# A fused attention and feed-forward block: the end of the last tile re-ordered, four shared head groups, and gb folded into the down weights

## The chip, the cores and the metric

The kernel runs on one core of a Trainium2 chip. A core has five engines that run their own instruction streams and wait for each other through semaphores: TensorE (PE; its weight loads are listed as PEld), VectorE (DVE), ScalarE (ACT), GpSimd (POOL) and SyncE (SP), whose queue (SPq) issues most of the DMA transfers; ACT has a DMA queue of its own (ACTq). Matmul results land in PSUM, eight banks of 128 x 512 fp32; all else is kept in SBUF. The metric is device time in microseconds (us) for one execution, and the median of several executions is compared.

## The reference

One sequence of 2048 tokens of 512 features, 32 heads of 16 features, a gated feed-forward part of width 1792:

```
mod = silu(c) @ w_mod              -> sa, ca, ga, sb, cb, gb   (512 each)
h = layernorm(x) * (1 + ca) + sa
q, k, v = h @ wqkv                 (32 heads of 16)
x = x + ga * (softmax(q k^T / 4) v) @ wo
h = layernorm(x) * (1 + cb) + sb
x = x + gb * ((gelu(h @ w_gate) * (h @ w_up)) @ w_down)
```

B_x is not used. Inputs and output are bf16; the layernorm's epsilon is 1e-5.

## The kernel before

**Work.** The 2048 queries are cut into seven sets of 512, 512, 256, 256, 256, 128 and 128 (`SETS`, numbered 0 to 6). The 32 heads form eight groups of four, called quads (`qd`). One unit of attention is a quad with the queries of a set; it runs over the 2048 keys in rounds, and each round gives four PSUM banks of scores, 512 columns each. All units together make 2048 banks. The exponential of every bank is taken either by ACT (tile `E`, one instruction for two or three banks of `ps_sc`) or, for some banks, by VectorE with a polynomial on integers (tiles `dt`, `dx`, `ed`, `mreg`, `qT`: a load of one bank out of PSUM, then six steps for one or two banks at a time). The product with the values accumulates in `ps_pv`; a column of ones in `vaug` yields the softmax's denominators.

**Units at the end.** Sets 5 and 6 have 128 queries each. Their first `QS` = 5 quads run as shared units of 256 queries; then come the remaining quads of set 5 alone, then those of set 6 alone. When a unit is done, `pv_done` copies the sums to `osb`. Its denominators normally go through DRAM (osb to `scr_den`, to `den`, a reciprocal in `rden`, to `scr_rec`, and broadcast back into `rb`), four DMAs on SP's queue, after which VectorE writes `onorm`. For the last quads of sets 5 and 6 the denominators are instead spread by a matmul with `self32`, and VectorE takes the reciprocal from PSUM (`near_end`, `tail_den`).

**Order.** The file is a recorder and a planner: `stream` walks through the score banks, keeps ACT fed, and places between them the products with the values, "side work" (`plan`, `next_side`: projections, the modulation vectors, the output projection `side_wo` and the feed-forward part `side_ffn` of finished sets) and VectorE's tasks (`task`, `step`). Waits and the order on each engine follow from this table of instructions. A bank goes to VectorE only under several conditions in `stream`, one of them an upper bound on `credit`, the amount of side work that is owed. Where PE has nothing to do, filler matmuls on `kme` and `ident` are issued.

**Feed-forward.** `side_ffn` handles a set's 14 slices of the width in chunks: for a set of 128 queries four chunks of 4, 4, 4 and 2 slices. A chunk is a gate product, an ACT step (Tanh in the stream, Gelu in the tail), an up product, and VectorE's product into `prodT` (in `hreg`). The down product sums 14 matmuls of 512 columns in one bank. `down_fin` multiplies the sum by the broadcast row `gb`, adds it to `xs`, and SP issues the output DMA of the tile. Of set 5, the first `EARLY` = 2 chunks are made in the stream.

**The tail.** After the last Exp, `tail` merges several generators by which is ready first: the last products with the values (`rest`), the denominators of the last quads, `tail_end` (set 6: output projection `wo_mm` on top of `xs`, layernorm statistics, rstd on POOL, the normalized tile in `dx`, four transposes, `modulate` on ACT and DVE into `wreg`, and its whole feed-forward part) and `tail_ffn` for what is left of set 5. In it the down products of set 5 go to `ps_pv`, those of set 6 to `ps_mi`.

The recorder makes an instruction that reads a PSUM bank wait for an earlier read of the same bank by another engine:

```python
                        elif kind == "ps":
                            for s, n in rd.items():
                                if s != eng:
                                    need(s, n, False)
```

## Time and profile before

| | us |
|---|---|
| median of 3 runs | 896.17 |
| lowest and highest of them | 896.01 and 898.0 |
| the profiled execution | 895.93 |
| its span, from the first to the last instruction | 894.2 |
| ACT busy | 865.8 |
| DVE busy | 816.4 |
| PE busy | 811.3 |
| POOL busy | 19.2 |
| ACT's last Exp starts | 870.97 |
| DVE's last instruction starts | 891.54 |

The granted clock of TensorE was 1.0 over the whole span. A row of the timeline gives the start, the time until the last of the row's instructions ends, the engine, the line, the operation and its output and inputs, how many there are, and in brackets how long the engine was idle before and for whom. A row that merges several pipelined instructions is shorter than their number times the duration of one. A row of the groups gives the busy time, the mean duration of one in ns, and the idle time before. In the order listings, a row is an instruction of one engine in program order, "xN" counts equal neighbours, and the brackets name the engines or DMA semaphores that it waits for.

### The profile page before, as it was taken

The page shows a single profiled execution, that of the slowest core. Times are in us where ns is not written, and L with a number is a line of the kernel's source. Part 1 is how long each engine was busy: PE and PEld are TensorE (multiplying, and loading weights), DVE is VectorE, ACT ScalarE, POOL GpSimd, SP SyncE. Part 2 cuts the span into 40 slices and gives each one's busy share as a digit, 9 for nine tenths or more (in the row PEclk, how much of TensorE's full clock was granted, in tenths as well). Part 3 has the DMA queues.
Part 4 walks back from the last instruction along what each step waited for, and adds up shares of the span by engine and source line. Part 5 has one row for each costly group of instructions (what it writes and reads, how often), then busy time and mean ns, then how long its engine had stood idle before and what let it go on. Part 6 is the DMA issues. An engine that isn't in the chain of part 4 may idle for free.

```text
span 894.2 us, 19936 instructions
## 1 busy us (share of the span) xinstructions
PE 811.3 (91%) x8661; PEld 286.7 (32%) x8661; DVE 816.4 (91%) x1500; ACT 865.8 (97%) x736; POOL 19.2 (2%) x36
## 2 busy tenths in 40 slices
PE   8899999988898898989999898999999999998998
PEld 3333222222222222222233222333333343334455
DVE  7778999999998999999998999998999999979955
ACT  4999999999999999999999999999999999999992
POOL 2100000000000000000000000000000000000000
PEclk9999999999999999999999999999999999999999
DMA  9012122000200000000000000010000000000100
GB/s 305 2 25 70 41 78 60 25 14 14 55 14 8 7 13 14 14 8 19 19 26 14 9 14 9 14 31 19 10 14 21 14 14 8 27 14 9 27 9 12
DMA packets 32509, 25.10 MB, mean 28 GB/s; under 512 B 16233, under 2 KB 28262, under 8 KB 32422
## 3 DMA queue, kind: packets, MB, share of 16 engines
q1 hardware_dynamic: 30566, 22.79, 8.6%
q8 instruction: 67, 1.10, 0.5%
q10 hardware_dynamic: 1856, 1.05, 0.4%
q14 instruction: 20, 0.16, 0.1%
HBM read 21.23 MB, written 2.61 MB: 27 GB/s over the span
## 4 chain that ended last, share of the span: by engine, by line
ACT 91%; PE 6%; DVE 2%; DMA 1%; issue 0%; SPq 0%
ACT E L321 88%; PE ps_sc L308 3%; ACT wreg L321 3%; PE ps_mi L308 2%; PE ps_pv L308 1%; DMA mreg<-in_w_mod_dram 1%; DVE st L361 0%; ACT hreg L321 0%; DVE dt L333 0%; DVE kmo L333 0%; DVE mreg L325 0%; DVE mreg L338 0%; SPq L371 0%; DVE hreg L325 0%; DVE wreg L338 0%
## 5 line engine op out<-in xcount | busy, mean ns | idle before, releaser
L321 ACT ACTIVATE E<-ps_sc 128x1536 bf16<-128x1536 f32 (+2 forms) x698 | 841.7, 1411 | 9.9 <-PE ps_sc L308 9.6
L308 PE MATMUL ps_sc<-qT,kme 32*128 32x256 bf16 (+2 forms) x1600 | 171.0, 304 | 13.8 <-ACT E L321 10.4
L308 PE MATMUL ps_sc<-qT,kmo 32*128 32x256 bf16 (+2 forms) x1664 | 172.2, 298 | 11.1 <-ACT E L321 7.9
L308 PE MATMUL ps_pv<-E,vaug 128*17 128x256 bf16 (+2 forms) x2884 | 179.8, 300 | 2.3 <-DVE osb L342 1.3
L333 DVE TENSOR_SCALAR dt<-ps_sc 128x512 int32<-128x512 f32 x204 | 139.0, 686 | 11.3 <-PE ps_sc L308 8.2
L308 PE MATMUL ps_sc<-kme,ident 128*128 128x512 bf16 x327 | 104.4, 384 | 36.9 <-ACT E L321 33.4
L308 PE MATMUL ps_mi<-wreg,mreg 128*128 128x256 bf16 (+2 forms) x624 | 123.6, 309 | 8.2 <-DVE wreg L342 4.0
L308 PEld LDWEIGHTS ps_sc<-qT,kmo 32*128 32x128 bf16 x1664 | 50.3, 92 | 120.2 <-ACT E L321 72.3
L308 PEld LDWEIGHTS ps_sc<-qT,kme 32*128 32x128 bf16 x1600 | 48.6, 92 | 125.2 <-ACT E L321 74.7
L308 PEld LDWEIGHTS ps_pv<-E,vaug 128*17 128x17 bf16 x2884 | 53.5, 88 | 96.8 <-issue 83.8
L325 DVE TENSOR_TENSOR qT<-qT,dx 128x1024 f16<-128x1024 f16 (+1 forms) x106 | 70.3, 664 | 1.3
L333 DVE TENSOR_SCALAR dx<-dt 128x1024 f16<-128x1024 uint16 (+1 forms) x107 | 70.0, 654 | 0.1
L308 PEld LDWEIGHTS ps_mi<-wreg,mreg 128*128 128x128 bf16 x624 | 47.7, 97 | 63.1 <-issue 30.1
L308 PE MATMUL ps_mi<-dreg,hreg 128*128 128x512 bf16 x210 | 65.3, 385 | 1.5 <-DVE wreg L338 0.8
L338 DVE SCALAR_TENSOR_TENSOR qT<-dt,qT 128x1024 int16<-128x1024 int32 (+1 forms) x53 | 62.3, 1176 | 0.1
L308 PEld LDWEIGHTS ps_sc<-kme,ident 128*128 128x128 bf16 x327 | 23.4, 97 | 88.1 <-ACT E L321 83.4
L325 DVE TENSOR_TENSOR ed<-ed,dx 128x1024 f16<-128x1024 f16 (+1 forms) x72 | 47.7, 662 | 0.7
L342 DVE CAST wreg<-ps_mi 128x512 bf16<-128x512 f32 x51 | 35.0, 686 | 11.3 <-PE ps_mi L308 10.8
L338 DVE SCALAR_TENSOR_TENSOR ed<-dt,ed 128x1024 int16<-128x1024 int32 (+1 forms) x36 | 42.2, 1172 | 0.2
L308 PE MATMUL ps_mi<-hreg,wreg 128*128 128x512 bf16 x120 | 38.7, 385 | 0.8 <-DVE vaug L342 0.5
L338 DVE SCALAR_TENSOR_TENSOR wreg<-wreg,ps_mi 128x512 bf16<-128x512 bf16 x51 | 34.7, 680 | 2.4 <-ACT wreg L321 1.8
L308 PE MATMUL ps_pv<-qT,vaug 128*17 128x256 bf16 (+2 forms) x178 | 36.5, 290 | 0.0
(126 smaller groups left out, 712.9 us busy)
## 6 DMA issues: line engine op xcount, KB each, us to landing
rb<-scr_rec SPq DMA_DIRECT2D x16, 256.0 KB
rb<-scr_rec SPq DMA_DIRECT2D x29, 128.0 KB
mreg<-in_w_mod_dram SPq DMA_DIRECT2D x1, 2048.0 KB, 12.9
out_dram<-xs SPq DMA_DIRECT2D x16, 128.0 KB, 1.7
mreg<-in_B_w_gate_dram SPq DMA_DIRECT2D x4, 448.0 KB, 7.2
mreg<-in_B_w_up_dram SPq DMA_DIRECT2D x4, 448.0 KB, 6.7
dreg<-in_B_w_down_dram SPq DMA_DIRECT2D x3, 512.0 KB, 7.6
wreg<-in_A_wqkv_dram SPq DMA_DIRECT2D x3, 384.0 KB, 9.8
```

The source lines that it names most:

```text
L308: return self.rec("pe", lambda e: e.matmul(out, lhsT, rhs, start=start, stop=stop, tile_position=tp), [lhsT, rhs], [out], cost=(n, int(rhs ...
L321: return self.rec("act", lambda e: e.activation(out, in_, func, scale=scale, **kw), rd, wr, cost=self.cost("act", out, [in_], "act" if bia ...
L325: return self.rec(eng, lambda e: e.tensor_tensor(out, a, b, op), [a, b], [out], cost=self.cost(eng, out, [a, b], "tt"))
L333: return self.rec(eng, lambda e: e.tensor_scalar(out, a, s1, s2, **kw), rd, [out], cost=self.cost(eng, out, [a], "ts" if len(rd) == 1 else ...
L338: return self.rec("dve", lambda e: e.scalar_tensor_tensor(out, a, s, b, op0=op0, op1=op1), rd, [out], cost=self.cost("dve", out, [a, b], " ...
L342: return self.rec(eng, lambda e: e.tensor_copy(out, in_), [in_], [out], cost=self.cost(eng, out, [in_], "ts"))
```

## The change

- `QS` goes from 5 to 4: four shared quads, so sets 5 and 6 have four units of their own each instead of three. `EARLY` goes from 2 to 3: three of the four chunks of set 5 are made in the stream.
- `gb` is multiplied into the down weights once (`scale_wd`, 7 VectorE instructions on `dreg`, a new entry of side work). `down_fin` then is one addition of the bank to `xs`; the tile `xw` is gone; 16 multiplications and 16 additions become 15 additions (the last tile has none).
- Banks may go to VectorE above the bound on `credit` where the next side work has nothing to issue.
- The tail: generators of set 6's chain and of set 5's down products are preferred by `FIRST` = 120 of the planner's ns until set 6's first Gelu, and put back by as much after it. The down products of set 5's first three chunks have a generator of their own (`tail_early`).
- In `tail_end` the epsilon is added by VectorE, POOL only does the power; the normalized tile is made from `xs` instead of the PSUM bank; the transposes alternate between two banks so that ACT reads one and VectorE the other.
- Set 6's down product is made in two halves of 256 columns in two banks (`ps_mi` and one of `ps_sc`); each starts with a matmul of `ident` with `xs`, so that the sum holds the residual. VectorE copies one half out and SP issues its DMA; ACT copies the other and issues its DMA on its own queue.

```diff
-QS = 5
+QS = 4
-EARLY = 2
+EARLY = 3
+FIRST = 120
...
+    def ln_pow(self, a, b):
+        r = self.rstd[:, a:b]
+        v, h = self.mv[:, a:b, 1], self.half[:, 0:b - a]
+        self.rec("pool", lambda e: e.tensor_tensor(r, v, h, ALU.pow), [v, h], [r], cost=self.cost("pool", r, [v], "pow"))
...
+    def scale_wd(self):
+
+        yield from self.until("wd")
+        if not self.dry:
+            self.task([lambda f=f: self.tt("dve", self.wd[:, f:f + 2, :], self.wd[:, f:f + 2, :],
+                                           self.gb[:, :].rearrange("p (o n) -> p o n", o=1).broadcast_to([P, 2, D]), ALU.mult)
+                       for f in range(0, NFC, 2)], "wds")
...
-            self.tt("dve", self.xs[:, t, :], self.xs[:, t, :], self.xw[:, :], ALU.add)
+            self.tt("dve", self.xs[:, t, :], self.xs[:, t, :], bank, ALU.add)
...
-        return [lambda: self.tt("dve", self.xw[:, :], bank, self.gb[:, :], ALU.mult), add]
+        return [add]
...
+        w.append((self.scale_wd, at(160), at(160)))
...
-                        and len(mem) == CH and slack > -100 and self.credit < (2600 if pos < ends[-3] else 1600)):
+                        and len(mem) == CH and slack > -100 and (self.credit < (2600 if pos < ends[-3] else 1600) or (pos >= ends[0] and self.next_side() is None))):
...
+            ahead = FIRST if ("g", kb, 0) not in self.have else -FIRST
...
-                    x = self.probe(nxt[i])
-                    if best is None or max(x, t + 30) < best[0]:
-                        best = max(x, t + 30), i
+                    x = max(self.probe(nxt[i]), t + 30)
+                    if best is None or x < best[0] - (ahead if i >= len(gens) - 2 else 0):
+                        best = x, i
...
-        self.task(self.ln2_steps(k, bank), ("ln2", k), self.after([("s2e", k)]), first=True)
+        v = self.mv[:, tile:tile + 1, 1]
+        steps = self.ln2_steps(k)
+        steps[0] = ("pool", lambda: self.ln_pow(tile, tile + 1))
+        self.task([lambda: self.ts("dve", v, v, EPS, None, ALU.add)] + steps, ("ln2", k), self.after([("s2e", k)]), first=True)
...
-        for h in range(2):
-            pb = f[1 + h]
-            yield lambda h=h, pb=pb: self.transp(pb, lambda t: self.normed(k, t), 1, h)
-            for i in range(2):
-                dc = 2 * h + i
-                self.modulate("act" if i == 0 else "dve", self.t2T[:, dc, c0:c0 + W],
-                              pb.bitcast(BF16)[:, W * i:W * i + W], self.modB, dc)
-        yield from self.tail_ffn(k, self.mi[:, :], f, 4, None)
+        pb = [f[1 + i].bitcast(BF16) for i in range(2)]
+
+        def trans():
+            for dc in range(NDC):
+                self.transpose(pb[dc % 2][:, W * (dc // 2):W * (dc // 2) + W], self.normed(k, 0)[:, P * dc:P * dc + P], self.ident[:, :])
+        yield trans
+        for dc in range(NDC):
+            self.modulate("act" if dc % 2 == 0 else "dve", self.t2T[:, dc, c0:c0 + W],
+                          pb[dc % 2][:, W * (dc // 2):W * (dc // 2) + W], self.modB, dc)
+        down = [self.mi[:, 0:D // 2], l[0][:, 0:D // 2]]
+        for i in range(2):
+            yield lambda i=i: self.mm(down[i], self.ident[:, :], self.xs[:, tile, D // 2 * i:D // 2 * i + D // 2], start=True, stop=False)
+        yield from self.tail_ffn(k, down, f, 4, None)
+
+    def tail_early(self, k, kb, down):
+        n = 512 // SETS[k][1]
+        yield from self.until(("osb", kb, 7))
+        for ci in range(EARLY):
+            yield from self.until(("prod", k, ci))
+            for fc in range(n * ci, min(NFC, n * ci + n)):
+                yield lambda fc=fc: self.down_mm(down, BCOL[k] // P, fc)
+        self.done(("early", k))
...
+        def fin(eng, i, queue, sem):
+            cols = slice(D // 2 * i, D // 2 * i + D // 2)
+            dst = self.xs[:, tile, cols]
+            if eng == "act":
+                self.act(dst, down[i], ACT.Copy)
+            else:
+                self.copy(eng, dst, down[i])
+            if self.probing is None:
+                self.dma(queue, self.out[0, P * tile:P * tile + P, cols], dst, sem)
+        self.task([lambda: fin("dve", 0, "sp", "out3")], None, first=True)
+        self.task([("act", lambda: fin("act", 1, "act", "out2"))], None, first=True)
```

Three places show how the instructions move. First PE after the last quad's denominators begin, before the change (`ps_sc<-wo,onorm` is the output projection of the last tile, `ps_pv<-dreg,hreg` the down product of set 5, `ps_sc<-wreg,mreg` gate and up products, `ps_sc<-ident,dx` the transposes):

```order
L308 MATMUL ps_sc<-wo,onorm 128x512 x2
L308 MATMUL ps_sc<-wo,onorm 128x512 [waits dve]
L308 MATMUL ps_sc<-osb,self 128x128 [waits dve]
L308 MATMUL ps_sc<-wo,onorm 128x512 [waits dve]
L308 MATMUL ps_pv<-dreg,hreg 128x512 x7
L308 MATMUL ps_sc<-wo,onorm 128x512 [waits dve]
L308 MATMUL ps_pv<-dreg,hreg 128x512
L308 MATMUL ps_sc<-wreg,mreg 128x128 x40
L308 MATMUL ps_sc<-wreg,mreg 128x128 [waits act]
L308 MATMUL ps_sc<-wreg,mreg 128x128 x7
L308 MATMUL ps_pv<-dreg,hreg 128x512 [waits dve]
L308 MATMUL ps_pv<-dreg,hreg 128x512 x3
```

And the same stretch of PE in the changed kernel:

```order
L309 MATMUL ps_sc<-wo,onorm 128x512 x2
L309 MATMUL ps_sc<-osb,self 128x128 [waits dve]
L309 MATMUL ps_sc<-wo,onorm 128x512 [waits dve]
L309 MATMUL ps_sc<-wo,onorm 128x512
L309 MATMUL ps_sc<-wreg,mreg 128x128 x16
L309 MATMUL ps_pv<-dreg,hreg 128x512
L309 MATMUL ps_sc<-wo,onorm 128x512 [waits dve]
L309 MATMUL ps_pv<-dreg,hreg 128x512 x11
L313 MATMUL ps_sc<-ident,dx 128x128 [waits dve]
L313 MATMUL ps_sc<-ident,dx 128x128 x3
L309 MATMUL ps_mi<-xs,ident 128x256
L309 MATMUL ps_sc<-xs,ident 128x256
```

The denominator matmul `ps_sc<-osb,self` stands one output projection earlier, 16 gate and up products of set 5 are left instead of 48, 11 of its down products stand between the last output projection and the transposes, and two matmuls with `xs` are new.

Second, VectorE at the same place, before (`st` and `mv` are the statistics of the last tile, `dx` its normalized rows, `hreg<-ps_sc,E` the products of set 5's chunks):

```order
L345 RECIPROCAL rb<-ps_sc 128x128 [waits pe]
L325 TENSOR_TENSOR onorm<-osb,rb 128x128 [waits dve]
L361 BN_STATS st<-ps_sc 128x6 [waits pe]
L364 BN_AGGR mv<-st 128x2 [waits dve]
L338 SCALAR_TENSOR_TENSOR hreg<-ps_sc,E 128x4x128 [waits act,pe]
L333 TENSOR_SCALAR dx<-ps_sc,mv,rstd 128x512 [waits pool,dve]
L338 SCALAR_TENSOR_TENSOR hreg<-ps_sc,E 128x2x128 [waits act,pe]
L333 TENSOR_SCALAR wreg<-ps_sc,modB 128x128 [waits act,pe] x2
```

and in the changed kernel:

```order
L343 COPY osb<-ps_pv 128x128 [waits pe]
L326 TENSOR_TENSOR onorm<-osb,rb 128x128 [waits d_dd5]
L346 RECIPROCAL rb<-ps_sc 128x128 [waits pe]
L326 TENSOR_TENSOR onorm<-osb,rb 128x128 [waits dve]
L339 SCALAR_TENSOR_TENSOR hreg<-ps_sc,E 128x2x128 [waits act,pe]
L362 BN_STATS st<-ps_sc 128x6 [waits pe]
L365 BN_AGGR mv<-st 128x2 [waits dve]
L334 TENSOR_SCALAR mv<-mv 128x1 [waits dve]
L334 TENSOR_SCALAR dx<-xs,mv,rstd 128x512 [waits pool,act]
L334 TENSOR_SCALAR wreg<-ps_sc,modB 128x128 [waits pe]
L334 TENSOR_SCALAR wreg<-ps_sc,modB 128x128
```

The short product of set 5 now stands ahead of the statistics and none between them and the normalization; the epsilon is new on VectorE; an `onorm` that waits for a DMA (`d_dd5`, the broadcast of quad 5's reciprocals) now stands between the copy of the last quad and its reciprocal.

Third, VectorE in the stream, after the last projection of the third 512 queries (`qT<-ps_mi`), where the scaling of the down weights stands in the changed kernel (`dt<-ps_sc` frees a score bank):

```order
L334 TENSOR_SCALAR qT<-ps_mi 128x512 [waits pe]
L334 TENSOR_SCALAR ed<-ed 128x1024 [waits dve]
L326 TENSOR_TENSOR dreg<-dreg,gb 128x1024 [waits d_wd0]
L326 TENSOR_TENSOR ed<-ed,dx 128x1024 [waits dve]
L343 COPY osb<-ps_pv 128x512 [waits pe]
L339 SCALAR_TENSOR_TENSOR ed<-dt,ed 128x1024 [waits dve]
L326 TENSOR_TENSOR dreg<-dreg,gb 128x1024
L326 TENSOR_TENSOR dreg<-dreg,gb 128x1024 [waits d_wd4]
L326 TENSOR_TENSOR dreg<-dreg,gb 128x1024
L326 TENSOR_TENSOR dreg<-dreg,gb 128x1024 [waits d_wd8]
L334 TENSOR_SCALAR dt<-ps_sc 128x512 [waits pe] x2
L326 TENSOR_TENSOR dreg<-dreg,gb 128x1024
```

Before the change two loads `dt<-ps_sc` followed directly on `ed<-ed`; now five scalings stand ahead of the next two loads, and with them a copy and two steps of the exponential that came after the loads.

41 lines of the change are left out of this document (28 added, 13 removed).

## The prediction

> **What bounds the kernel now.** I read the page's busy shares first, then the chain of waits, then ACT's groups from the start of the steady stream (18 us) to the end of the last Exp (872.6 us).
>
> ```profile
> PE 811.3 (91%) x8661; PEld 286.7 (32%) x8661; DVE 816.4 (91%) x1500; ACT 865.8 (97%) x736; POOL 19.2 (2%) x36
> ACT 91%; PE 6%; DVE 2%; DMA 1%; issue 0%; SPq 0%
> L321 ACT ACTIVATE E<-ps_sc 128x1536 bf16<-128x1536 f32 x459 | 650.4, 1555 | 1.4 <-PE ps_sc L308 1.1
> L321 ACT ACTIVATE E<-ps_sc 128x1024 bf16<-128x1024 f32 x231 | 244.3, 1150 | 0.2 <-PE ps_sc L308 0.2
> 204.52 1.23 DVE L338 SCALAR_TENSOR_TENSOR ed<-dt,ed 128x1024 int16<-128x1024 int32 x1
> 867.50 0.51 ACT wreg L321
> ```
>
> Three engines are busy over 90%, but only ACT carries the chain, and in that stretch it idles 1.4 + 0.2 = 1.6 us of 854. So the program has two parts: a stream that lasts as long as ACT's instructions, and a tail of 894.2 - 872.6 = 21.6 us in which no Exp is left. The stream shortens only by less ACT work. The tail:
>
> ```profile
> L308 PE MATMUL ps_sc<-wreg,mreg 128*128 128x128 bf16 x160 | 9.9, 219 | 0.3 <-DVE wreg L333 0.2
> 870.97 1.58 ACT L321 ACTIVATE E<-ps_sc 128x1536 bf16<-128x1536 f32 x1
> 873.23 0.82 PE L308 MATMUL ps_sc<-wo,onorm 128*128 128x512 bf16 x3
> 873.35 0.29 DVE L342 COPY osb<-ps_pv 128x128 f32<-128x128 f32 x1
> 873.88 0.38 PE L308 MATMUL ps_sc<-osb,self 128*128 128x128 f32 x2
> 874.31 0.96 DVE L345 RECIPROCAL rb<-ps_sc 128x128 f32<-128x128 f32 x1 [0.47 <-PE ps_sc L308]
> 874.32 1.67 PE L308 MATMUL ps_pv<-dreg,hreg 128*128 128x512 bf16 x7
> 875.30 0.29 DVE L325 TENSOR_TENSOR onorm<-osb,rb 128x128 bf16<-128x128 f32 x1
> 875.83 0.38 PE L308 MATMUL ps_sc<-wo,onorm 128*128 128x512 bf16 x1
> 876.25 0.70 DVE L361 BATCH_NORM_STATS2 st<-ps_sc 128x6 f32<-128x512 f32 x1 [0.66 <-PE ps_sc L308]
> 876.98 0.18 DVE L364 BATCH_NORM_AGGREGATE mv<-st 128x2 f32<-128x6 f32 x1
> 877.25 0.22 POOL L565 TENSOR_SCALAR rstd<-mv 128x1 f32<-128x1 f32 x1 [17.74 <-DVE mv L364]
> 877.56 0.58 POOL L566 TENSOR_TENSOR rstd<-rstd,half 128x1 f32<-128x1 f32 x1
> 878.25 0.69 DVE L338 SCALAR_TENSOR_TENSOR hreg<-ps_sc,E 128x512 bf16<-128x512 f32 x1 [1.09 <-PE ps_sc L308]
> 878.86 0.80 DVE L333 TENSOR_SCALAR dx<-ps_sc,mv,rstd 128x512 bf16<-128x512 f32 x1
> 879.87 0.39 PE L312 MATMUL ps_sc<-ident,dx 128*128 128x128 bf16 x4
> 880.18 0.81 ACT L321 ACTIVATE wreg<-ps_sc,modB 128x128 bf16<-128x128 bf16 x2 [1.10 <-PE ps_sc L312]
> 880.75 0.69 DVE L333 TENSOR_SCALAR wreg<-ps_sc,modB 128x128 bf16<-128x128 bf16 x2 [0.76 <-PE ps_pv L308]
> 881.50 3.58 PE ps_sc L308 x61
> 889.32 1.46 PE L308 MATMUL ps_mi<-dreg,hreg 128*128 128x512 bf16 x6
> 890.82 0.69 DVE L325 TENSOR_TENSOR hreg<-ps_mi,gb 128x512 bf16<-128x512 f32 x1 [0.83 <-PE ps_mi L308]
> 891.54 0.42 DVE L325 TENSOR_TENSOR xs<-xs,hreg 128x512 bf16<-128x512 bf16 x1
> 891.99 0.34 SPq L371 DMA_DIRECT2D out_dram<-xs  x1
> ```
>
> To be seen: the chain is last values, copy, denominator, reciprocal, `onorm`, output projection, statistics, rstd, normalization, transposes, modulation, then PE without a break to 890.8, and two VectorE instructions and a DMA. Set 5's leftovers sit in it twice: seven down products hold the last output projection from 875.6 to 875.83, and a product into `hreg` holds the normalization from 878.14 to 878.86. From one matmul to the next it is 3.58 / 61 = 0.059 us at 128 columns, and (1.67 - 0.38) / 6 = 0.215 us at 512.
>
> **The change part by part, the tail.** I hold the end of the last Exp at 872.55 and walk down the chain with the order of the changed program. The durations that the rows above do not have:
>
> ```profile
> L333 DVE TENSOR_SCALAR rm<-rm x1: 153/153/153, 2.5 to 2.5; 128x1 f32<-128x1 f32 x1
> 859.62 0.41 DVE L333 TENSOR_SCALAR hreg<-xs,mv,rstd 128x512 bf16<-128x512 bf16 x1 [0.40 <-POOL rstd L566]
> 820.40 1.05 PE L308 MATMUL ps_mi<-wreg,mreg 128*128 128x256 bf16 x8
> L342 DVE COPY osb<-ps_pv 128x256 f32<-128x256 f32 x29 | 12.2, 422 | 2.4 <-PE ps_pv L308 1.8
> L321 ACT ACTIVATE E<-ps_sc 128x256 bf16<-128x256 f32 x2 | 0.8, 384 | 2.2 <-PE ps_sc L308 2.2
> 0.78 0.44 ACTq L371 DMA_DIRECT2D xs<-in_A_x_dram  x1
> ```
>
> *Denominator to statistics.* The denominator matmul stands one output projection earlier, so it starts when the copy is done, at 873.69 instead of 873.88; the reciprocal starts at 874.12, and `onorm` ends at 875.40. PE meanwhile issues two output projections (to 874.35), 16 gate and up products (0.94, to 875.29) and one down product (to 875.50); then the last output projection, 0.33 earlier than 875.83. The short product of set 5 ahead of the statistics needs those 16 matmuls and 0.4 us and is over at about 875.95, so the statistics gain 0.30.
>
> *Statistics to normalization.* Before: 876.25 to 879.66, 3.41 us. Now: statistics and aggregate 0.91, a gap of 0.03, the epsilon on VectorE 0.15, the gap to POOL 0.09 (877.16 to 877.25), the power 0.58, a gap of 0.10, the normalization out of SBUF 0.41 instead of 0.80 out of PSUM: 2.27 us, a gain of 1.14. The ACT copy of `xs`, on which it now waits, has 512 columns; by the two Exp forms that is 1.555 - 2 x 0.405 = 0.75 us, and it starts with the end of the statistics at 876.65, so it ends 0.3 us ahead of the power. The normalization ends at 878.22.
>
> *Transposes.* Before, they waited for down products until 879.87. Now 11 down products follow the last output projection, 11 x 0.215 = 2.37 us from 875.72 to 878.09, just ahead of 878.27, when the transposes can start. The lead is 1.60. With this little room, three more down products would have cost 0.5 us.
>
> *Modulation.* Before, each VectorE step waited for ACT's read of the same bank; from the first transpose to a full stream of matmuls it took 881.50 - 879.87 = 1.63. With two banks ACT's pair (0.81, its start 0.06 later, since it waits for the third transpose) and VectorE's pair (0.69) run side by side; 0.31 + 0.06 + 0.81 + 0.05 = 1.23. Lead 2.0. The two matmuls with `xs` and two down products (0.65 together) fit into this wait.
>
> *PE to the end.* 62 instead of 61 matmuls follow, 0.06. The down products become 28 of 256 columns at (1.05 - 0.27) / 7 = 0.111: 3.11 instead of 14 x 0.215 = 3.01; bounded below by half of 0.215, no cost. Lead 1.85. A check from the other side: PE is hardly idle in the tail, and what left it is one chunk of set 5, 32 of the 160 gate and up products, 32 x 0.059 = 1.9 us. The two sums agree.
>
> *Last steps.* Before, 891.96 - 890.82 = 1.14 from PE to the end of VectorE. Now the last half is read by ACT in 0.38 at about 888.97, to 889.36; VectorE's half is complete two matmuls earlier and ends before it. Lead 2.60. The DMA leaves ACT's queue, 0.44 to issue against 0.34 on SP's: 2.5 us gained at the end.
>
> **The stream.** Counted in the two programs, ACT has three Exp of 1536 fewer and three of 1024 more, since VectorE takes 207 banks instead of 204: 3 x (1.555 - 1.150) = 1.22 us less; one Tanh of 512 columns moves in from the tail, for 0.51 us in the chain. That is 0.7 us gained. It is hidden by nothing and comes if ACT stays as full as before. VectorE pays with three more banks and seven scalings, and is rid of 16 multiplications like the one at 890.82.
>
> ```profile
> L325 DVE TENSOR_TENSOR wreg<-wreg 128x1024 bf16<-128x1024 bf16 x46 | 31.4, 683 | 0.2
> 200.00:225.00 25.00, 22.12 (x160) 5.80 (x160) 24.34 (x41) 25.00 (x22) 0.00 (x0) 1.00 0.04 12
> ```
>
> The scalings stand at about 202 us, where VectorE is busy 24.34 of 25 us. At 0.683 they are 4.8 us; what the multiplications give back (0.69 each) comes later. If one with a broadcast operand ran like the slowest 1024-column row shown (1.23), it would be 8.6 us. The table of instructions allows for the shorter price, and I take that; its cover is the loads of score banks that the planner moved, and without that cover ACT waits for held banks.
>
> No row here has a broadcast operand. The Trainium skill, "VectorE: DVE Perf Modes", section "What auto-detection actually checks", gives the faster two-source mode wherever all tensors are 16-bit with a step of one; by it the scaling stays at 4.8, by the other price the sum would be 3.8 us longer at most.
>
> I take the idle time of ACT as unchanged at 1.6 us, bounded by a gain of 1.3 (the waits for PE in the two rows of Exp) and a loss of 4.8 (the scaling without cover). **Sum:** 2.5 + 0.7 = 3.2 us. The profiled execution took 895.93, 0.24 below the median of 896.17, so 892.7 profiled and **893.0** as a median.
>
> **The rivals.**
>
> *The stream gives some of it back.* All from 202 us on is planned anew, with less room on VectorE; a bank loaded late is a PE wait and an ACT gap. Against it: 1.6 us of idle time in 854 in a schedule of the same make. For it: 1.3 of those 1.6 us were waits for PE, so PE has no room at some places. At 2 to 5 us of new idle time: 895 to 898, 896 as its middle.
>
> *VectorE falls behind at the scaling (slower).* At 202 us five scalings stand ahead of two loads that free score banks. If they come at 1.23 and their cover fails altogether, 8.6 us appear on ACT: 901.6. It decides against the change from 5.9 us on, where 893.0 passes 896.17 + 2.7. Against it: VectorE catches up wherever its banks are given out under the planner's conditions.
>
> *Quad 5's reciprocals come too late.*
>
> ```profile
> 864.99 0.17 DVE L345 RECIPROCAL rden<-den 128x4 f32<-128x4 f32 x1
> 867.27 0.52 SPq L371 DMA_DIRECT2D rb<-scr_rec  x1
> 871.91 0.28 DVE L325 TENSOR_TENSOR onorm<-osb,rb 128x128 bf16<-128x128 f32 x1
> ```
>
> Before, the reciprocal ran 2 us ahead of quad 6's copy, and 6.9 us passed to the `onorm`. Now it follows that copy, so at about 867.3 (the copy's place among the last banks is the same), and the `onorm` at 873.6 stands ahead of the last quad's reciprocal: 6.3 us for the two DMAs and the wait between them. If they need all that they had before, VectorE waits about 0.7 us, and all behind it: 893.7. I expect no wait, since `onorm` did not have to wait at 871.91.
>
> *The halves cost more than their columns.* The 14 additional matmuls load weights again. If none of that were hidden, each at the most the 0.059 in which a matmul passes with its load at 128 columns, 0.8 us would go: 893.8. The row at 820.40, eight different weights, speaks against it.
>
> The Trainium skill, "TensorE: Matmul & The Clock Gate", section "Back-to-back issue gap", states a sustained spacing with weight loads of about 81 ns at 128 columns and 131 ns at 512, so that halving a matmul costs more than nothing (estimate from that page, about 0.9 us here). This trace shows 59 and 215 ns.
>
> **How the numbers follow.** Forecast 62%, with its own range of 891.6 to 894.3; the stream gives back 22%; quad 5 late 5%; halves dear 3%; VectorE behind 8%. This kernel's measurement can tell about 0.3%, 2.7 us, so faster means below 893.48: most of the forecast, 54%. Within: the rest of it (8%), the two small rivals (8%) and 20 of the 22%: 36%. Slower: 10%. The range 891.5 to 896.6 leaves out the far part of the stream's rival (6%), the slower one (8%) and a little of the forecast below.
>
> **What would show it.** Right: the last Exp ends within 1 us of 871.9, and from there to the span's end it is about 19 us instead of 21.6; statistics to normalization 2.3 us; transposes to the full stream of matmuls 1.2; PE's end to the start of the last output DMA 0.5. ACT idle from 18 us to the last Exp at about 1.6 us. Wrong: ACT idle of more than 3 us there, above all after 202 us; a wait of VectorE for a DMA ahead of the last reciprocal; scalings of over 1 us; a tail above 20 us.

## The result and the profile after

In the comparison on one chip the changed kernel took 894.2 us (median of 9 executions, 893.28 to 896.15) against 896.46 us for the kernel before (9 executions, 896.01 to 898.22): a ratio of 0.9971 with a 95% interval of 0.9961 to 0.9982. It is faster by 2.3 us; the forecast was 893.0 with a range of 891.5 to 896.6. The profiled execution of the changed kernel is its slowest one: span 894.4, 896.15 us. So first: what of that belongs to the change?

The page's busy shares and chain of the changed kernel, and ACT's two steady groups from 21 us to the end of the last Exp (columns: busy time in all, mean ns of one, idle time before, releaser):

```profile
PE 786.5 (88%) x8673; PEld 293.3 (33%) x8805; DVE 823.7 (92%) x1521; ACT 865.2 (97%) x737; POOL 18.7 (2%) x35
ACT 87%; PE 9%; DVE 3%; DMA 1%; issue 0%; SPq 0%
L322 ACT ACTIVATE E<-ps_sc 128x1536 bf16<-128x1536 f32 x455 | 646.1, 1557 | 2.5 <-PE ps_sc L309 2.2
L322 ACT ACTIVATE E<-ps_sc 128x1024 bf16<-128x1024 f32 x234 | 247.3, 1147 | 0.2 <-PE ps_sc L309 0.2
```

ACT still carries the chain, but its idle time there is 2.5 + 0.2 = 2.7 us, where it had been 1.4 + 0.2. The 0.2 us stand ahead of the first Exp of these rows in both kernels; inside the stream it is 2.5 against 1.4.

The start (timeline, then 2-us windows; columns of the windows: busy time of PE, PEld, DVE, ACT and POOL with instruction counts, granted clock, DMA share, GB/s):

```profile
10.20 0.94 PE L309 MATMUL ps_sc<-sc_bf,mreg 128*128 128x1 bf16 x32 [1.90 <-DMA mreg<-in_w_mod_dram]
11.43 1.67 PE L313 MATMUL ps_sc<-ident,dreg 128*128 128x128 bf16 x16
21.05 1.02 ACT L322 ACTIVATE E<-ps_sc 128x1024 bf16<-128x1024 f32 x1 [0.25 <-PE ps_sc L309]
...
10.00:12.00 2.00, 1.73 (x41) 1.60 (x43) 0.49 (x3) 0.00 (x0) 0.00 (x0) 0.92 1.10 345
12.00:14.00 2.00, 2.00 (x14) 1.23 (x12) 0.94 (x2) 1.55 (x2) 0.00 (x0) 0.50 1.10 337
14.00:16.00 2.00, 1.87 (x6) 0.61 (x5) 0.09 (x1) 0.69 (x1) 0.00 (x0) 0.73 1.12 335
```

The same rows of the kernel before:

```profile
8.71 0.94 PE L308 MATMUL ps_sc<-sc_bf,mreg 128*128 128x1 bf16 x32 [0.33 <-DMA mreg<-in_w_mod_dram]
9.94 1.05 PE L312 MATMUL ps_sc<-ident,dreg 128*128 128x128 bf16 x16
18.52 4.79 ACT L321 ACTIVATE E<-ps_sc 128x1024 bf16<-128x1024 f32 x4 [0.25 <-PE ps_sc L308]
```

The 1024-column Exp at which ACT's steady stream is taken to begin (called the first one below, though one ran before it) comes 21.05 - 18.52 = 2.53 us later: the first part of `w_mod` landed 1.5 us later, and then the granted clock fell to 0.5, so that 16 transposes took 1.67 us instead of 1.05. The program is the same up to there, so this is not the change. I measure from that Exp instead. **Stream**, from it to the end of the last Exp: before 18.52 to 872.55, 854.03; after 21.05 to 875.50, 854.45: 0.42 longer, where 0.70 less was forecast. **Tail**, from there to the span's end: before 21.65, after 18.90: 2.75 shorter, where 2.5 was forecast. Without the late start, 2.75 - 0.42 = 2.33 us are gained, as the medians say.

The tail of the changed kernel (timeline), to be held against the tail in the prediction:

```profile
873.80 1.69 ACT L322 ACTIVATE E<-ps_sc 128x1536 bf16<-128x1536 f32 x1
876.27 0.29 DVE L343 COPY osb<-ps_pv 128x128 f32<-128x128 f32 x1
876.61 0.49 PE L309 MATMUL ps_sc<-osb,self 128*128 128x128 f32 x2
877.14 0.96 DVE L346 RECIPROCAL rb<-ps_sc 128x128 f32<-128x128 f32 x1 [0.38 <-PE ps_sc L309]
878.48 0.39 PE L309 MATMUL ps_sc<-wo,onorm 128*128 128x512 bf16 x1
878.71 2.54 PE L309 MATMUL ps_pv<-dreg,hreg 128*128 128x512 bf16 x10
878.91 0.70 DVE L362 BATCH_NORM_STATS2 st<-ps_sc 128x6 f32<-128x512 f32 x1
879.86 0.15 DVE L334 TENSOR_SCALAR mv<-mv 128x1 f32<-128x1 f32 x1
880.09 0.56 POOL L571 TENSOR_TENSOR rstd<-mv,half 128x1 f32<-128x1 f32 x1 [23.35 <-DVE mv L334]
880.76 0.41 DVE L334 TENSOR_SCALAR dx<-xs,mv,rstd 128x512 bf16<-128x512 bf16 x1 [0.75 <-POOL rstd L571]
881.23 0.40 PE L313 MATMUL ps_sc<-ident,dx 128*128 128x128 bf16 x4
881.61 0.81 ACT L322 ACTIVATE wreg<-ps_sc,modB 128x128 bf16<-128x128 bf16 x2 [1.31 <-PE ps_sc L313]
881.66 0.59 DVE L334 TENSOR_SCALAR wreg<-ps_sc,modB 128x128 bf16<-128x128 bf16 x2 [0.49 <-PE ps_sc L313]
891.66 0.42 DVE L343 CAST xs<-ps_mi 128x256 bf16<-128x256 f32 x1 [0.63 <-PE ps_mi L309]
891.88 0.38 ACT L322 ACTIVATE xs<-ps_sc 128x256 bf16<-128x256 f32 x1 [1.37 <-PE ps_sc L309]
892.29 0.36 ACTq L372 DMA_DIRECT2D out_dram<-xs  x1
```

The down products stand behind the last output projection and none holds it (eleven in the program, ten of them with a record); they end at 881.25, just as the transposes start. ACT and VectorE modulate side by side from 881.61, and the halves end with VectorE at 892.08 and ACT at 892.26.

### The profile page after: what moved, and what is told of

It is laid out like the page before. It is cut to its first block, busy times and chain, and to the rows that moved or that the text cites. A ratio compares the mean times of both kernels' runs of the same rounds, so it can differ in the third digit from the quotient of the medians.

```text
span 894.4 us, 20126 instructions
## 1 busy us (share of the span) xinstructions
PE 786.5 (88%) x8673; PEld 293.3 (33%) x8805; DVE 823.7 (92%) x1521; ACT 865.2 (97%) x737; POOL 18.7 (2%) x35
## 4 chain that ended last, share of the span: by engine, by line
ACT 87%; PE 9%; DVE 3%; DMA 1%; issue 0%; SPq 0%
ACT E L322 84%; PE ps_sc L309 4%; PE ps_mi L309 3%; ACT wreg L322 3%; PE ps_pv L309 1%; DMA mreg<-in_w_mod_dram 1%; DVE dt L334 0%; DVE wreg L339 0%; PE ps_sc L313 0%; DVE st L362 0%; DVE dx L334 0%; DVE qT L334 0%; DVE wreg L343 0%; DVE kmo L334 0%; DVE osb L343 0%
## 5 line engine op out<-in xcount | busy, mean ns | idle before, releaser
L309 PE MATMUL ps_sc<-qT,kmo 32*128 32x256 bf16 (+2 forms) x1664 | 170.1, 298 | 15.2 <-ACT E L322 10.5
L334 DVE TENSOR_SCALAR dt<-ps_sc 128x512 int32<-128x512 f32 x207 | 141.0, 685 | 11.3 <-PE ps_sc L309 8.5
L309 PE MATMUL ps_sc<-kme,ident 128*128 128x512 bf16 x274 | 90.2, 384 | 46.2 <-ACT E L322 43.8
L309 PE MATMUL ps_mi<-wreg,mreg 128*128 128x256 bf16 (+2 forms) x637 | 117.7, 301 | 8.4 <-DVE wreg L339 3.4
L326 DVE TENSOR_TENSOR qT<-qT,dx 128x1024 f16<-128x1024 f16 (+1 forms) x112 | 74.0, 660 | 1.1
L309 PEld LDWEIGHTS ps_mi<-wreg,mreg 128*128 128x128 bf16 x656 | 50.3, 97 | 56.3 <-issue 26.8
L339 DVE SCALAR_TENSOR_TENSOR qT<-dt,qT 128x1024 int16<-128x1024 int32 (+1 forms) x56 | 65.4, 1169 | 0.1
L309 PE MATMUL ps_mi<-dreg,hreg 128*128 128x512 bf16 (+1 forms) x183 | 56.3, 376 | 2.7 <-issue 2.2
L309 PE MATMUL ps_pv<-qT,vaug 128*17 128x256 bf16 (+2 forms) x186 | 38.9, 291 | 0.0
L309 PE MATMUL ps_mi<-hreg,wreg 128*128 128x512 bf16 x111 | 36.0, 385 | 1.1 <-issue 0.5
```

What stands on the lines that cost most here:

```text
L309: return self.rec("pe", lambda e: e.matmul(out, lhsT, rhs, start=start, stop=stop, tile_position=tp), [lhsT, rhs], [out], cost=(n, int(rhs ...
L326: return self.rec(eng, lambda e: e.tensor_tensor(out, a, b, op), [a, b], [out], cost=self.cost(eng, out, [a, b], "tt"))
L334: return self.rec(eng, lambda e: e.tensor_scalar(out, a, s1, s2, **kw), rd, [out], cost=self.cost(eng, out, [a], "ts" if len(rd) == 1 else ...
L339: return self.rec("dve", lambda e: e.scalar_tensor_tensor(out, a, s, b, op0=op0, op1=op1), rd, [out], cost=self.cost("dve", out, [a, b], " ...
```

## The experiments

Single times are not compared below 0.3%; stretches inside a profile are. "Idle" is the idle time of ACT inside the stream, from its first Exp on, which is that of the 1536-column group: 1.4 us before, 2.5 us after.

### The tail, part by part

**e1_chain_back** takes the edits of the last tile's chain back: epsilon on POOL, normalization out of the bank, transposes in two groups that share a bank between the engines.

```diff
-        steps = self.ln2_steps(k)
-        steps[0] = ("pool", lambda: self.ln_pow(tile, tile + 1))
-        self.task([lambda: self.ts("dve", v, v, EPS, ...)] + steps, ...)
+        self.task(self.ln2_steps(k, bank), ("ln2", k), ...)
-        yield trans
+        for h in range(2): ...
```

> The changed kernel with the last tile's chain as it was: epsilon on POOL, normalization out of the PSUM bank, transposes in two groups so that ACT and VectorE read the same bank. Everything else, the moved chunk too, stays. Theory (the tail is one chain, PE has little left beside it): statistics to normalization takes 0.91 + 0.09 + 0.22 + 0.09 + 0.58 + 0.10 + 0.80 = 2.8 us instead of 2.26, the modulation 0.4 us more, so the time from the last Exp's end to the span's end goes from 18.9 to 19.8 us. Rival (the tail is PE's work, and the gain came from the chunk that left it): it stays at 18.9 within 0.2. ACT's stream (from its fourth Exp to the end of the last) stays at 854.4.

Measured: tail 19.85, so the chain edits are worth 0.95 us. One time: 896.04.

**e2_one_end** takes the two halves back.

```diff
-        down = [self.mi[:, 0:D // 2], l[0][:, 0:D // 2]]
+        down = [self.mi[:, :]]
...
```

> The changed kernel with the last tile's down product in one bank of 512 columns, one VectorE copy and one DMA on SP's queue (the residual still comes in by a matmul). Theory: the last copy is 0.69 instead of 0.38 and the DMA twice as large, so last Exp to span's end is 19.2 to 19.3 us instead of 18.9. Rival (two engines halve the end of 1.14 us by themselves): 19.6 or more.

Measured: tail 19.26, so 0.36 us. One time: 895.56.

**e3_chunk_back** takes the split of set 5 back: five shared quads, and two chunks of set 5 made in the stream instead of three.

```diff
-QS = 4
+QS = 5
-EARLY = 3
+EARLY = 2
```

> The changed kernel with five shared quads and two early chunks, as before; all else of the change stays. Theory: 32 gate and up products come back into the tail, 32 x 0.059 = 1.9 us, of which PE's short waits beside the chain take 0.3 to 0.6: last Exp to span's end 20.2 to 20.8 us instead of 18.9. Rival (the chain alone sets the tail, PE hides the chunk): 19.2 or less. In the stream, counted: one Exp of 1536 fewer, one of 1024 more, one Tanh of 512 fewer, 0.9 us less for ACT. If four shared quads cost the 1.1 us of new idle time of ACT, the stream is 852.4; if the new plan as a whole does, 853.5.

Measured: stream 853.54 with an idle time of 2.5 us, so the four quads do not cost the idle time (ACT and VectorE go through the same instructions as in the changed kernel up to 812 us); tail 21.04, a little above what was expected: 2.14 us more than with the smaller chunk. One time: 895.82.

**e5_chunk_alone** joins e1 and e2, so that the chunk and the VectorE banks are left, and with them the folding of `gb`, the residual that comes in by a matmul, and the preference `FIRST` with `tail_early`.

> The changed kernel with the last tile's chain, its order on PE and its single end as before (512-column down products, one output DMA); what stays is the smaller last chunk of down-weight work (four shared quads, gb in the weights) and the extra VectorE banks. Undone one at a time, the chain cost 0.95 us of tail and the single end 0.36 us; without the chunk, chain and end together gained 0.61 us against the kernel before. Theory (PE's room decides: the chain's gain is there only because the chunk has left PE): the tail from the end of the last Exp is 18.90 + 0.95 + 0.36 = 20.2 us. Rival (the parts are independent): 18.90 + 0.61 = 19.5 us. The stream, from the first 1024-column Exp to the end of the last Exp, 853.5 to 854.5 us if the granted clock stays at 1.0, about 1.4 us more if it drops to 0.5 somewhere in it.

Measured: last Exp ends at 874.60 of a span of 894.8, a tail of 20.2, as the theory had it. The stream, 855.89, has the fall of the clock in it that is dealt with below. One time: 896.63. So the chunk alone shortens the tail by 21.65 - 20.2 = 1.45 us, chain and end without the chunk by 21.65 - 21.04 = 0.61, and all together by 2.75: 0.69 us are there only because each makes room for the other. "Alone" is not quite alone, since e3 and e5 both keep the folding, the residual and the preference. The end of e5 shows what that is worth:

```profile
891.86 0.69 DVE L343 CAST xs<-ps_mi 128x512 bf16<-128x512 f32 x1 [0.83 <-PE ps_mi L309]
892.57 0.34 SPq L372 DMA_DIRECT2D out_dram<-xs  x1
```

One VectorE step leads to the DMA instead of two, 0.71 us instead of the 891.99 - 890.82 = 1.17 of the kernel before. So of the 1.45 us some 1.0 are the chunk's (an estimate from these rows), and what each makes room for is rather more than 0.69. In e3 the statistics start 3.95 us after the last Exp's end instead of 3.41, and a product of set 5 on VectorE holds the normalization until 879.58, so the old chunk is in the chain's way on VectorE as well as on PE.

### The stream

**e4_no_extra** takes the additional VectorE banks back.

```diff
-                        and (self.credit < (...) or (pos >= ends[0] and self.next_side() is None))):
+                        and self.credit < (2600 if pos < ends[-3] else 1600)):
```

> The changed kernel without the extra banks for VectorE while side work waits. Counted: seven Exp of 1536 more and seven of 1024 fewer, so ACT has 7 x 0.405 = 2.8 us more. Theory: the stream goes from 854.4 to 857.2 and ACT's idle time stays near 2.7 us. Rival (the extra banks crowd VectorE and made the idle time): the stream is 856.1 with the idle time back at 1.6. The tail stays at 18.9.

Measured: stream 857.95, idle 2.9. ACT has 464 and 228 Exp instead of 457 and 235, 7 x (1.557 - 1.147) = 2.9 us of Exp, and 0.4 us more of idle time. One time: 898.16. The banks are worth 3.5 us of the stream; without them it is 3.9 us longer than in the kernel before, more than the tail gains. So the idle time doesn't come from the banks either.

**e8_other_order** asks whether the idle time is an accident of the order.

```diff
-SOON = 100
+SOON = 110
```

> The changed kernel with one constant of the planner (SOON, the time ahead of its due time at which side work counts as soon due) at 110 instead of 100: ACT has the same 457, 235, 3 and 2 Exp of 1536, 1024, 512 and 256 columns, in another order, and nothing else differs. Theory (the 1.1 us of idle time of ACT that the change added are an accident of the order): the idle time in the rows of Exp comes out elsewhere than 2.7 us, anywhere from 1.4 to 3.5, and the stream from the first 1024-column Exp to the end of the last Exp follows it one for one, 853.1 to 855.3 us. Rival (the changed rules bring that idle time with them: less room for PE and VectorE): 2.7 us within 0.3 again, and the stream 854.2 to 854.8 us. The tail is 18.9 us either way.

Measured: idle 2.7 (with what stands ahead of the stream, as the expectation counts it, 2.9 instead of 2.7), first Exp at 20.16, last Exp's end at 875.13: a stream of 854.97. The stream is inside the theory's range and 0.2 us above the rival's, but only 0.2 of its 0.5 us are idle time, so it does not follow that one for one; for the idle time the rival holds. By stretches the waits stand elsewhere (1.1 us at 780 to 810 us after the first Exp, where the changed kernel has none), and their sum is nearly the same. Eleven executions: 893.71 to 895.79, median 894.51; ratio to the kernel before 0.9982 (0.9973 to 0.9991).

**e11_before_other_order** does the same to the kernel before.

> The kernel before with SOON at 105 instead of 100: another order of everything after the first 100 us under the old rules, with two Exp more of 1536 and two fewer of 1024 columns. Theory (the 1.6 us of idle time of ACT in the kernel before were a favourable order, not a property of the old rules): 2.2 to 3.2 us of idle time in the rows of Exp, as in every order of the changed rules so far (2.5 to 3.0). Rival (the changed rules bring the added idle time with them): 1.3 to 1.9 us.

```profile
L321 ACT ACTIVATE E<-ps_sc 128x1536 bf16<-128x1536 f32 x460 | 652.3, 1552 | 1.7 <-PE ps_sc L308 1.4
L321 ACT ACTIVATE E<-ps_sc 128x1024 bf16<-128x1024 f32 x228 | 241.4, 1145 | 0.0
```

These are ACT's groups of that kernel: 1.7 us inside the stream. With the 0.2 ahead of it, as the expectation counts, it is 1.9 to 2.0, at the upper end of the rival's range, which holds narrowly. The stream of 855.2 is the 0.8 us of Exp more and 0.3 of idle time. One time: 897.8. So two orders under the old rules have 1.4 and 1.7 us, and the changed rules have 2.5 in the changed kernel and these in e3, e4 and e8:

```profile
L322 ACT ACTIVATE E<-ps_sc 128x1536 bf16<-128x1536 f32 x454 | 644.9, 1553 | 2.5 <-PE ps_sc L309 2.2
L322 ACT ACTIVATE E<-ps_sc 128x1536 bf16<-128x1536 f32 x462 | 656.4, 1568 | 2.9 <-PE ps_sc L309 2.7
L322 ACT ACTIVATE E<-ps_sc 128x1536 bf16<-128x1536 f32 x455 | 647.0, 1563 | 2.7 <-PE ps_sc L309 2.3
```

What all orders under the changed rules have in the stream, and none of the old ones, is the folding of `gb` into the down weights. **e12_fold_alone** puts that alone into the kernel before, with another start, which is read apart (there the last tiles of x also move as in e6, and one warm-up matmul goes).

```diff
+        w.append((self.scale_wd, at(160), at(160)))
...
-        return [lambda: self.tt("dve", self.xw[:, :], bank, self.gb[:, :], ALU.mult), add]
+        return [add]
...
-        self.dma(sp, self.wmod[:, :, 0:1024], wmv[:, :, 0:1024], "wm0")
+        for i, q in enumerate((sp, act)):
+            self.dma(q, self.wmod[:, 2 * i:2 * i + 2, 0:1024], wmv[:, 2 * i:2 * i + 2, 0:1024], "wm0%d" % i)
```

> Two edits of the kernel before in stretches that do not touch, read apart in its profile. First, of the parts of the change only the folding of gb: the seven scalings of the down weights at about 200 us, down products that wait for them, and no multiplication with gb behind the down products; five quads, no extra VectorE banks, the old chain and the old end. ACT has two Exp more of 1536 and two fewer of 1024 columns (0.8 us). Theory (of what the five orders under the changed rules had in common, with 2.4 to 3.0 us of idle time of ACT against 1.6 and 1.7 in two orders under the old rules, the folding is what brings it): 2.3 to 3.0 us of idle time in the rows of Exp, the stream 855.6 to 856.2 us. Rival (it is none of the folding's, but of several parts together): 1.4 to 1.9 us, the stream 854.7 to 855.1 us. The tail loses the multiplication of 0.69 us at its end: 20.9 to 21.0 us. Second, the start: the first part of w_mod in two halves, one on each queue, ahead of w_qkv, and the last tiles of x behind the third load of x. Theory (the executions' spread at a full clock is the landing of w_mod behind 384 KB of w_qkv): w_mod's matmuls start at 8.3 to 8.6 us and the executions at a clock of 1.0 lie within 0.7 us of each other, where those of the kernel before spread over 1.8 us (895.55 to 897.37 us). Rival (it lands when it lands): a spread of 1.5 us or more again.

ACT's groups, the scalings, and the place of the longest wait (groups, then timeline):

```profile
L321 ACT ACTIVATE E<-ps_sc 128x1536 bf16<-128x1536 f32 x459 | 652.6, 1568 | 2.4 <-PE ps_sc L308 2.2
L321 ACT ACTIVATE E<-ps_sc 128x1024 bf16<-128x1024 f32 x228 | 241.5, 1151 | 0.0
L325 DVE TENSOR_TENSOR dreg<-dreg,gb x7: 681/682/686, 201.3 to 208.6; 128x1024 bf16<-128x1024 bf16 x7
...
570.81 1.47 PE L308 MATMUL ps_mi<-dreg,hreg 128*128 128x512 bf16 x6
571.89 1.22 DVE L338 SCALAR_TENSOR_TENSOR qT<-dt,qT 128x1024 int16<-128x1024 int32 x1
573.16 0.28 PE L308 MATMUL ps_pv<-qT,vaug 128*17 128x256 bf16 x1 [0.67 <-DVE qT L338]
573.48 0.40 PE L308 MATMUL ps_sc<-qT,kme 32*128 32x256 bf16 x6
573.92 1.45 ACT L321 ACTIVATE E<-ps_sc 128x1536 bf16<-128x1536 f32 x1 [0.97 <-PE ps_sc L308]
```

Idle 2.4 us and a stream from 17.78 to 873.82, 856.04: with the same numbers of Exp as e11 the folding costs 0.7 us of idle time and 0.84 of the stream, at scalings of 0.682 us. Against the kernel before, whose order on ACT and VectorE it shares up to 201 us, it is 1.0 us of idle time. It is no further order, though: up to about 810 us ACT and VectorE go through the same instructions as in e4. So what is compared is three orders with the folding (the changed kernel and e3, e4 and e12, e8) at 2.4 to 2.9 us and two without it at 1.4 and 1.7. The longest wait can be read off: six down products run on PE, the next product waits 0.67 us for a VectorE bank, the scores stand behind it on PE, and ACT waits 0.97 us for them. Why the folding lets down products gather there was not tried; that they now wait for nothing but PE's turn, with one addition instead of two VectorE steps behind them, is an argument. The tail was 21.4, not 20.9: VectorE's multiplication is gone from the end, but VectorE's last addition, which waits for PE, starts 18.50 instead of 18.27 us after the last Exp. Eleven executions: median 897.72 (896.9 to 898.25), ratio to the kernel before 1.001 (1.0001 to 1.0019). That interval all but reaches 1, and the start is another; by stretches the folding alone loses, 2.0 us in the stream, 0.8 of them Exp, against 0.25 gained in the tail.

### The start and the clock

**e6_x4_behind** moves one load, since the late landing stood beside it (and issues one warm-up matmul fewer).

```diff
-        self.dma(act, self.xs[:, 12:16, :], xv[:, 12:16, :], "x4")
+        self.dma(sp, self.xs[:, 12:16, :], xv[:, 12:16, :], "x4")
```

> The changed kernel with the load of the last four tiles of x moved from ACT's queue to SP's, behind the third load of x, and one warm-up matmul fewer. Theory (in the profiled execution of the changed kernel the first part of w_mod landed late beside that load, PE then paused for 1.9 us, and the clock fell to 0.5): w_mod's matmuls start at 8.3 to 8.7 us without waiting more than 0.5 us, the first 1024-column Exp starts at 18.2 to 18.6 us, no granted clock under 0.9 ahead of 20 us, and the median comes to 892.6 to 893.3 us, with fewer executions near 895.5 than the 4 of 9 of the changed kernel. Rival (the landing of w_mod does not depend on the other queue, or what was moved is missed later): the first Exp at 18.5 to 21 us as before, the median 893.3 to 894.5 us.

Measured: `w_mod`'s matmuls at 8.43, first Exp at 18.24, no fall ahead of 20 us, as the theory had it in the profile; but the median of eleven executions was 894.72 (893.29 to 894.99): five were at a mean clock of 0.998 (the expectation of e9 counts six), and two at a clock of 1.0 took 894.9 as well. The profile shows where the clock fell, in 2-us windows:

```profile
500.00:502.00 2.00, 1.47 (x10) 0.62 (x12) 2.00 (x5) 2.00 (x3) 0.00 (x0) 1.00 0.05 17
502.00:504.00 2.00, 1.08 (x9) 0.30 (x9) 2.00 (x4) 2.00 (x3) 0.00 (x0) 1.00 0.00 0
504.00:506.00 2.00, 2.00 (x17) 0.36 (x16) 2.00 (x4) 1.90 (x2) 0.00 (x0) 0.56 0.00 0
506.00:508.00 2.00, 2.00 (x17) 0.37 (x16) 0.48 (x2) 1.40 (x2) 0.00 (x0) 0.59 0.04 8
```

PE has little to do at 502 us, the clock falls at 504 for (0.44 + 0.41) x 2 / 0.5 = 3.4 us, and ACT waits 1.1 us for scores. The stream is 855.94, 1.5 us longer than without. e1, e2 and e5 had the same fall at the same place.

**e7_cold_start** makes a pause on purpose.

```diff
-        self.warm_up(16)
+        self.warm_up(6)
```

> The changed kernel with 6 instead of 16 warm-up matmuls ahead of w_mod's; the order of everything else is the same. PE then has nothing for at least 2 us ahead of w_mod's matmuls. Theory (a weak stretch of PE lets the granted clock fall): the profile shows a clock near 0.5 for about 3 us between 8 and 16 us, the 16 transposes take 1.7 instead of 1.05 us, the first 1024-column Exp starts 1 to 2.5 us later than 18.5, and all executions are longer than 893.3 by that, so a median of 894.3 to 896. Rival (the drops come whatever PE does): drops in no more executions than the 4 of 9 seen, median 893.3 to 894.2 us.

Measured: clock 0.5 from 9.8 to 13.2 us, transposes 1.69 us, first Exp at 19.19, nine of ten executions at a mean clock under 1.0. Median 896.77 (894.29 to 898.96): above what the theory had. One fall of 3.4 us at half clock is 3.4 x 0.5 / 893 = 0.002 of the mean; the five longest executions stood at 0.994, so about three falls each. Where the further ones stand, no profile here shows.

**e9_hole_filled** adds two filler matmuls at 502 us to e6's kernel.

```diff
                     self.mm(self.scp[:, s0, :], *filler)
+                    if 498200 < t < 498300:
+                        self.spare(self.scp[:, s0, :], 2)
```

> The kernel of e6_x4_behind with two more filler matmuls of 512 columns where PE has little to do at about 502 us (four instead of two); the order of everything else is the same. Theory (the fall of the granted clock at 504 us, which six of eleven executions of e6_x4_behind had, comes from that hole of PE): no granted clock under 0.9 between 100 and 890 us, the mean clock 1.0 in at least ten of eleven executions, the median 893.2 to 893.6 us, and the idle time of ACT from the first 1024-column Exp on 2.4 to 2.6 us instead of 3.6. Rival (the clock falls in some execution or other, wherever it can): the fall moves to another weak place (569, 647 or 824 us), some five of eleven executions at 894.5 to 895, the median 894 to 894.8 us.

The same stretch of that kernel, which ran 2.4 us later (windows, then the fillers):

```profile
502.00:504.00 2.00, 1.76 (x22) 0.60 (x10) 2.00 (x5) 2.00 (x2) 0.00 (x0) 1.00 0.12 41
504.00:506.00 2.00, 1.57 (x11) 0.42 (x10) 2.00 (x4) 2.00 (x3) 0.00 (x0) 1.00 0.00 0
506.00:508.00 2.00, 1.73 (x23) 0.55 (x23) 2.00 (x5) 2.00 (x3) 0.00 (x0) 1.00 0.00 0
...
504.41 1.04 PE L309 MATMUL ps_sc<-kme,ident 128*128 128x512 bf16 x4 [0.21 <-ACT E L322]
10.89 0.94 PE L309 MATMUL ps_sc<-sc_bf,mreg 128*128 128x1 bf16 x32 [2.04 <-DMA mreg<-in_w_mod_dram]
```

Eleven of twelve executions were at a clock of 1.0, and idle is 2.5 instead of 3.7. A clock of 1.0 in six of e6's eleven executions and in eleven of these twelve points to the hole as what lets the clock fall there. It does not decide alone: the changed kernel has the same order, its largest pause of PE there is 0.92 us as in e6, and its profile keeps the clock (the two windows around the pause, at 505.70):

```profile
504.00:506.00 2.00, 1.49 (x13) 0.33 (x9) 2.00 (x4) 2.00 (x3) 0.00 (x0) 1.00 0.00 0
506.00:508.00 2.00, 1.37 (x17) 0.44 (x17) 2.00 (x4) 2.00 (x3) 0.00 (x0) 1.00 0.00 0
```

The median of e9, 894.37 (893.1 to 895.79), is not lower, for the other reason: the last row of the view before shows `w_mod` late again, with the last tiles of x behind it. So what e6 said of the start was luck, and its theory is wrong there.

**e10_other_order_x4** joins e6's start and e8's order.

> The kernel of e8_other_order (SOON at 110) with the load of the last four tiles of x behind the third on SP's queue, as in e6_x4_behind. Theory: e8 had no fall of the clock in eleven executions, but its start depends on when w_mod lands (893.71 to 895.79 us); with the start fixed at 18.2 us the stream of 854.97 us and the tail of 18.9 us give a span of 892.1 and 893.7 to 893.9 us with a spread under 0.6 us. Rival (the order has its own weak places and only was lucky): some executions at a clock of 0.998 and 895 us. If both this and e9_hole_filled come out as their theories say, e9_hole_filled is the faster by 0.4 us, since its order holds ACT idle for 0.5 us less.

Measured: span 892.1 as worked out; median of twelve 893.99, nine of them from 893.59 to 895.15 at a clock of 1.0, three at 0.998 and 896.1 to 896.53. The rival holds: this order has its weak places too. None of e6, e9 and e10 can be told from the changed kernel by its median.

In e12 `w_mod` came in two halves ahead of `w_qkv`: its matmuls ran at 7.82 without a wait, and all eleven executions had a clock of 1.0, but they spread over 1.35 us, in two groups (896.9 to 897.25, 897.72 to 898.25). That is neither the 0.7 of the theory nor the 1.5 of the rival. What makes the two groups stays open.

## Why the prediction was right, point by point

The time lies in the range, and the tail's mechanism came out as worked; but the range of 891.5 to 896.6 also held no change at all, and the stream went the other way from the forecast. By the prediction's own split 894.2 is "within" (36%) and not "faster", which was below 893.48 (54%). Of its signs, the tail of 18.9, 2.26 us from statistics to normalization, 882.47 - 881.23 = 1.24 from transposes to the full stream of matmuls and 0.45 from PE's end to the last DMA came; the last Exp's end within 1 us of 871.9 did not (875.50, where the start makes 2.53 of the 3.6 us), nor idle time at 1.6, and none of the signs of being wrong did.

- *The tail's chain.* Each lead but the last came within 0.1 us of its working. Measured against the end of the last Exp: last output projection 0.30 earlier (0.33), statistics 0.29 (0.30), statistics to normalization 3.41 to 2.26 (2.27), transposes 1.59 (1.60), full stream of matmuls 1.98 (2.0), PE to the last half 1.89 (1.85), end of the last engine 2.65 (2.60), span 2.75 (2.5). Most of the 0.25 at the end is the last DMA: on ACT's queue it issues in 0.36 us, not 0.44, and from there to the span's end it is 1.75 us, before 1.87.
- *Why it fits together.* The check from the other side, that PE is hardly idle in the tail and that the chunk that left it is most of the gain, was half right: the chunk without the chain's edits gives 1.45 of 2.75, folding included, and it also makes room for them (0.69 us or more of both).
- *The scalings.* 0.681 us each, 204.5 to 211.8 us, in the changed kernel, so the price of 4.8 us was taken rightly, and VectorE didn't fall behind there: the slower rival is refuted. The trace agrees with what the Trainium skill, "VectorE: DVE Perf Modes", section "What auto-detection actually checks", gives for 16-bit tensors, here with a broadcast operand.
- *The halves.* 256-column products follow each other in 0.11 us; no cost beyond the columns.
- *Quad 5.* The `onorm` at 876.47 stood right behind its copy without a wait. With five quads (e3) and without the banks (e4) it waited for its DMA, 0.42 and 1.35 us, off the chain.
- *The step that failed: "I take the idle time of ACT as unchanged at 1.6 us".* It was 2.7. The 0.7 us fewer of ACT work came as counted (three Exp less of one kind, three more of the other, one Tanh), but 1.1 us of new idle time took more than that. The rival for it, 2 to 5 us of new idle time, was too large. Its path, a late bank of VectorE, then PE, then ACT, is that of e12's longest wait; but the less room on VectorE that it named does not come from the additional banks, since e4 without them idles no less, nor from the scalings themselves, beside which ACT does not wait. The runs showed the folding in its place: inside the stream, idle time is 2.4 to 2.9 us in three orders with it and 1.4 and 1.7 in two without, and folding alone brings it in the one order that was tried (e12); how it does so stays open. So 3.2 us of forecast gain became 2.3.
- *The median.* 894.2 instead of 893.0: 0.9 of the 1.2 us are that idle time net of the tail (3.2 - 2.3); the other 0.3 is the kernel before, whose median is 896.46 here and was 896.17 in the three runs from which the forecast started. The start and the clock spread the executions: four of nine executions stood at a clock of 0.998, 895.19 to 896.15; the five at 1.0 reach from 893.28 to 894.2.

## What to carry to other kernels

When a tail is both a chain and a full engine, shorten both: here the smaller chunk without chain and end gave 1.45 us, chain and end without it 0.61, and all of them 2.75. Moving work ahead is not free because an engine has room on average: take one part of a change alone and read the idle time of the engine that bounds, order by order, before calling the rest "unchanged". And measure inside a profile from the first steady instruction, since the start alone moved by 2.5 us between two executions that begin with the same instructions.

## What the hardware showed that I had not expected

The granted clock of PE fell to half without a long pause of PE (0.92 us at most). In e6 it fell after 4 us in which PE was busy for 1.47 + 1.08 us, and stayed at half for 3.4 us; two more fillers there kept it at 1.0 in eleven of twelve executions. The Trainium skill, "TensorE: Matmul & The Clock Gate", section "What's actually happening", says that a free-running window of about 3.4 us decides, and that half rate follows an idle one. The length and the half agree with these runs; that the window has to be idle does not: a thinly used one was enough, and not each time (e9's profile shows a wait of 2.04 us at the start and no fall behind it, and the changed kernel's profile keeps the clock around the pause at which e6's loses it). What the threshold is, no run here shows.

The first 1024-column Exp follows `w_mod`'s matmuls at a fixed distance while the clock holds: 8.43 to 18.24 (e6), 8.71 to 18.52 (before), 10.89 to 20.70 (e9), 9.81 us each time (in e12, where they run earliest, 7.82 to 17.78, 9.96). Where PE waits for that one load of 1 MB, issued at 1.7 us, its landing decides when the whole stream begins (a wait of 0.33 us before, 1.90 after, 2.04 in e9), and it took from 6.6 us (e6) to 9.1 us (e9) in two profiles with the same loads in the same queues.
